# An attention block with two MLPs behind it on one core: plain scores in the first unit, earlier loads for the second, and scores between value products

## The chip, the core and the metric

The kernel runs on one core of a Trainium2 chip. The metric is the time of one execution in microseconds (us) on the device. TensorE (PE) multiplies matrices, VectorE (DVE), ScalarE (ACT) and GpSimd (POOL) work element by element, and SyncE (SP) issues most of the transfers between memory and the on-chip buffer.

## The reference, cut to what matters

Two batches of eight heads, 576 tokens, 64 columns a head, all in float32. The bias of the scores comes out of a small network over a function of the two positions. Two MLPs follow.

```
S = 576
scores = (1/8) * q @ k.T
x = log1p(|i - j|) / log1p(max(i, 1))
bias = relu(x @ w1 + b1) @ w2
attn = softmax(scores + bias)
out = attn @ v
x = out.reshape(1152, 512)
x = (silu(x @ w_gate) * (x @ w_val)) @ w_out
y = softplus(x @ w_in) @ w_out2
```

## The kernel before, in words

Every engine runs in the order in which the program is written (`manual_schedule` over all five), so the place of a line in the loops is its place in the queue of its engine. A product of more than one pass splits its operands into a rounded high part and the remainder, the low part (`high`, `low`, L185 to L191), and the products of the parts are added up.

**The bias stretch.** A loop over 36 rows of blocks makes the bias for all heads. `hidden(i)` writes four tiles `r` = relu of a slice of the table `G`, three on DVE and one on ACT (L256, L258). `second` multiplies them on PE into `pb` (L266). `keep` copies `pb` on ACT to a staging tile `st`, of which there are four, and SP stores it into the bias tiles, 288 KB a row (L278, L282; the first four rows in two halves each, L285). From row 6 on each turn of the loop also takes one step of the preparation of the first unit's K and Q (`prepare_k`, `prepare_q`: a cast, then a subtraction of the high part). At rows 23, 26, 31 and 33 (`EARLY`) it runs a slot of the attention loop.

**The attention loop.** A unit is a pair of heads of one batch; there are eight. A unit has nine slots, four for its first 256 queries (`sub` 0) and five for the other 320 (`sub` 1), and the fifth chunk mixes rows of both heads (`mix`). `run_slot` does this in order: `scores` of the slot's chunk on PE (four matmul instructions, L303); `gather`, the copies of an earlier slot's transposes out of PSUM; `biased` on DVE, which adds the bias and takes the extremum (L324); `softmax` of the chunk before (exp on ACT, L338; sums and reciprocals on DVE, L342, L343; the normalisation on POOL, L346); two steps of preparation for the next unit; `transposes` on PE (L373); and, when the last piece of an earlier sub is gathered, `values` of all its pieces in one burst on PE (L400: 20 matmul instructions for `sub` 0, 30 for `sub` 1). The transposes of a sub follow three slots behind its last scores (`LAG`).

**Loads.** `load_k` and `load_qv` issue a unit's loads on SP, with K and Q each copied twice, so that the two heads of a pair fill 128 rows. Those of the first unit stand ahead of the stretch. The second unit's K loads at the first slot (row 23), its Q and V at slot 4, the first one behind the stretch. The two mix tiles `m0`, `m1` are made behind the stretch, and POOL clears their last 64 columns (L551); they lie where buffers of the stretch were, so each memset waits for what last used its place.

Of the kernel before, what the change touches and what calls it, by code (L numbers as in the profile page):

```python
# [11 lines left out]
F32 = mybir.dt.float32  # L12
# [7 lines left out]
P = 128  # L20
# [9 lines left out]

BATCHES = ((0,), (1, 2), (3,)), ((0, 1), (2, 3), (4,))
# [7 lines left out]
EARLY = (23, 26, 31, 33)  # L39

# [58 lines left out]
def tile_kernel(ctx: ExitStack, tc, qT, kT, vS, wb, wg, wv, wo, wi, wo2, table, out):  # L99
# [4 lines left out]

    nc.scalar.preload_act_table_set("exp_and_others")
# [11 lines left out]
    slots(xp, "a", ("B11", "T1", "B21", "B22"))  # L117
# [7 lines left out]
    with ExitStack() as actx:  # L125
# [30 lines left out]
        def load(r, src, pr, b):  # L156
            for d in range(2):
                sp.dma_start(
                    out=r[D * d : D * (d + 1)], in_=src[b, 2 * pr : 2 * pr + 2].rearrange("h d s -> d h s")
                )  # L160

        def load_k(i):

            pr, b = UNITS[i]
            kr = bias[0][:, :2] if i > 2 else rawp.tile([P, 2, S], F32, tag="kr", name="kr")
            load(kr, kT, pr, b)
            return dict(i=i, pr=pr, b=b, kr=kr)

        def load_qv(u):
            pr, b = u["pr"], u["b"]  # L170
            if u["i"] == 1:
                u["qr"] = pairs[5].rearrange("p (a s) -> p a s", a=2)
            else:
                u["qr"] = qraw.tile([P, 2, S], F32, tag="qr", name="qr")
            load(u["qr"], qT, pr, b)
# [29 lines left out]

        def prepare_q(u, sub):
# [6 lines left out]
            sm = smp.tile([P, 4, 5], F32, name="sm")  # L213
            if sub == 0:
                parts = [(0, 0, 0, 256), (1, 256, 0, 256)]
                chunks = [(0, 0), (1, 0), (0, 1), (1, 1)]
            else:
# [3 lines left out]
                chunks = [(0, 0), (1, 0), ("mix",), (0, 1), (1, 1)]  # L221
            u[sub] = dict(u, sub=sub, qh=qh, ql=ql, chunks=chunks, sm=sm, es=[], last=[], at={})
# [52 lines left out]
        def keep(s, pb):  # L275
            c, t = divmod(s, 8)
            st = stp.tile([P, S], F32, name="st")
# [8 lines left out]

        def scores(u, n):

            sub, pr, kst = u["sub"], u["pr"], u["kst"]
# [9 lines left out]

            parts = [(t, a, o) for t in ("ql", "qh") for a, o in heads]  # L300
# [107 lines left out]
        def finish(u):  # L408

            if u["i"] == 4 and u["sub"] == 0:  # L410
# [46 lines left out]
        load_qv(units[0])  # L457
        chunks = [(i, sub, n) for i in range(2 * NP) for sub in range(2) for n in range(4 + sub)]
        jobs, turned, gathered, done, spare = [], [], [], [], itertools.cycle([False, True])
        prep = itertools.chain(prepare_k(units[0]), prepare_q(units[0], 0))  # L460
        before = None
        slot = 0

        def run_slot():
            nonlocal turned, done, prep, before, slot
            if slot < len(chunks):
                i, sub, n = chunks[slot]
                if n == 0:
                    for _ in prep:
                        pass  # L470
                    if sub == 0:
                        if i + 1 < 2 * NP:
                            units.append(load_k(i + 1))
# [38 lines left out]
            for _ in range(len(gathered) if last_job else max(ends, default=0)):  # L512
# [11 lines left out]
        with tc.manual_schedule(engines={E.PE, E.Activation, E.DVE, E.Pool, E.SP}):  # L524
# [7 lines left out]
            for i, s in enumerate(order):  # L532
# [6 lines left out]
                if i > 5:  # L539
                    next(prep, None)  # L540
# [7 lines left out]
            pairs[2:] = pairs[3:] + pairs[2:3]  # L548
# [528 lines left out]
```

## Time and profile before

| | |
|---|---|
| median of three runs | 601.92 us (600.58 to 603.95) |
| profiled execution | 600.55 us, its span 598.5 us |
| PE busy | 582.8 us, 97% of the span |
| DVE, ACT, POOL busy | 460.3, 376.2, 111.5 us |
| DMA | 63.30 MB, mean 106 GB/s |
| bias stretch | to about 64 us |
| attention with its last value burst | to 197.01 us |

The span is the time between the first and the last instruction in the profile of the one execution; the rest of its 600.55 us lies around it. Busy shares are means over all of it: the two MLPs, from 197 us on, are long rows of matmuls, and the attention part ahead of them is where the engines wait for each other.

### The profile page before, as it was taken

Reading aid. Unit: us, or ns where it says so; the run is one execution under the profiler, and the core shown is the slowest. Engines: PE = TensorE matmul, PEld = TensorE weight load, DVE = VectorE, ACT = ScalarE, POOL = GpSimd, SP = SyncE. Lnnn points to the kernel's source line nnn. Section 1 sums busy time; section 2 is a strip of 40 time slices with the busy share of each in tenths; the row PEclk is TensorE's granted clock in tenths of the full one; section 3 lists DMA queues with packets and bytes.
Section 4 is the critical chain, followed back from the end, with each engine's and each line's share of the span. In section 5 each row is a group of like instructions: output and inputs, shape, how many; then the busy total and the mean of one; then the engine's idle time right before and its main releaser. Section 6 shows DMA issues by size and latency. Waiting matters only on the chain.

```text
span 598.5 us, 11379 instructions
## 1 busy us (share of the span) xinstructions
PE 582.8 (97%) x4274; PEld 516.7 (86%) x4274; DVE 460.3 (77%) x982; ACT 376.2 (63%) x715; POOL 111.5 (19%) x165
## 2 busy tenths in 40 slices
PE   8899799999999999999999999999999999999997
PEld 6343588888887999999999999999989989988986
DVE  7999578878888999897689735679998976983432
ACT  5998787879888876665558424349835734732520
POOL 0301587878993000000000000000000000000000
PEclk9999999999999999999999999999999999999999
DMA  8979923334432333324225222122444240400012
GB/s 221 207 197 208 214 63 99 91 110 111 110 119 89 117 98 108 103 75 137 73 79 190 84 71 71 71 75 70 138 130 134 90 141 5 137 36 1 2 51 106
DMA packets 47414, 63.30 MB, mean 106 GB/s; under 512 B 4480, under 2 KB 35200, under 8 KB 47360
## 3 DMA queue, kind: packets, MB, share of 16 engines
q1 hardware_dynamic: 47360, 62.59, 36.7%
q8 instruction: 33, 0.54, 0.4%
q14 instruction: 21, 0.17, 0.1%
HBM read 49.60 MB, written 2.36 MB: 87 GB/s over the span
## 4 chain that ended last, share of the span: by engine, by line
PE 81%; DVE 7%; ACT 4%; DMA 4%; issue 2%; POOL 2%; SPq 0%; DVEq 0%; ACTq 0%; POOLq 0%
PE pw L684 37%; PE pw L992 16%; PE pw L635 13%; PE ps L303 5%; PE po L400 5%; PE pt L373 4%; DVE r L258 3%; DMA bias<-st 2%; ACT st L278 1%; DMA e<-in_qT_dram 1%; ACT r L256 1%; POOL ql L191 1%; PE pb L266 1%; ACT e L338 1%; DMA G<-in_table_dram 1%
## 5 line engine op out<-in xcount | busy, mean ns | idle before, releaser
L992 PE MATMUL pw<-oh,g2h 128*128 128x512 f32 x144 | 56.2, 390 | 0.0
L992 PE MATMUL pw<-oh,g2l 128*128 128x512 f32 x144 | 56.1, 390 | 0.0
L992 PE MATMUL pw<-ol,g2h 128*128 128x512 f32 x144 | 56.1, 389 | 0.0
L303 PE MATMUL ps<-kst,ql 128*128 128x288 f32 x160 | 49.3, 337 | 4.5 <-POOL ql L191 3.4
L266 PE MATMUL pb<-r,wb_sb 128*32 128x288 f32 x576 | 49.1, 412 | 4.4 <-ACT st L278 2.7
L258 DVE TENSOR_SCALAR r<-G 128x576 f32<-128x576 f32 x108 | 51.5, 553 | 0.1
L635 PE MATMUL pw<-gh,sh 128*128 128x384 f32 x144 | 48.4, 336 | 0.0
L635 PE MATMUL pw<-gh,sl 128*128 128x384 f32 x144 | 48.4, 336 | 0.0
L635 PE MATMUL pw<-gl,sh 128*128 128x384 f32 x144 | 48.3, 336 | 0.0
L266 PEld LDWEIGHTS pb<-r,wb_sb 128*32 128x32 f32 x576 | 20.3, 109 | 31.5 <-ACT st L278 11.5
L609 DVE SCALAR_TENSOR_TENSOR x<-raw,x 128x512 int32<-128x512 int32 x68 | 46.2, 686 | 0.9
L303 PEld LDWEIGHTS ps<-kst,ql 128*128 128x128 f32 x160 | 29.0, 188 | 16.3 <-DVE sm L324 5.7
L303 PE MATMUL ps<-kst,qh 128*128 128x288 f32 x160 | 42.6, 294 | 0.0
L324 DVE CUSTOM_DVE_ANT_0 e<-ps,bias 128x576 f32<-128x576 f32 x44 | 33.0, 749 | 9.0 <-PE ps L303 7.6
L346 POOL TENSOR_SCALAR e<-e,sm 128x576 f32<-128x576 f32 x44 | 34.1, 784 | 25.2 <-DVE sm L343 19.4
L380 ACT COPY at<-pt 128x512 f32<-128x512 f32 (+2 forms) x69 | 36.2, 547 | 3.6 <-PE pt L373 3.4
L338 ACT ACTIVATE e<-e,sm 128x576 f32<-128x576 f32 x44 | 34.3, 780 | 6.1 <-DMA vt<-in_vS_dram 3.4
L400 PE MATMUL po<-at,v 128*64 128x256 f32 (+3 forms) x384 | 36.8, 332 | 1.0 <-DVE at L380 0.8
L1030 DVE TENSOR_TENSOR acc<-pw,acc 128x512 f32<-128x512 f32 x27 | 17.5, 684 | 25.1 <-PE pw L992 25.1
L606 DVE TENSOR_SCALAR x<-x 128x512 int32<-128x512 int32 x68 | 28.7, 426 | 9.2 <-ACT x L605 5.0
L400 PEld LDWEIGHTS po<-at,v 128*64 128x64 f32 x384 | 26.6, 137 | 8.0 <-issue 1.7
L992 PEld LDWEIGHTS pw<-oh,g2l 128*128 128x128 f32 x144 | 27.0, 188 | 5.8
(272 smaller groups left out, 1678.2 us busy)
## 6 DMA issues: line engine op xcount, KB each, us to landing
raw<-in_wo_dram SPq DMA_DIRECT2D x28, 512.0 KB, 3.6
bias<-st SPq DMA_DIRECT2D x32, 288.0 KB, 4.7
raw<-in_wi_dram SPq DMA_DIRECT2D x16, 512.0 KB, 3.8
raw<-in_wv_dram SPq DMA_DIRECT2D x12, 512.0 KB, 4.2
raw<-in_wg_dram SPq DMA_DIRECT2D x12, 512.0 KB, 3.5
qr<-in_qT_dram SPq DMA_DIRECT2D x14, 288.0 KB, 4.1
v<-in_vS_dram SPq DMA_DIRECT2D x8, 384.0 KB, 3.4
bias<-in_kT_dram SPq DMA_DIRECT2D x10, 288.0 KB, 4.2
```

The costliest lines, as they stand in the source:

```text
L258: nc.vector.tensor_scalar(r, G[:, w0 : w0 + S], PB[:, n : n + 1], 0.0, op0=ALU.add, op1=ALU.max)
L266: nc.tensor.matmul(pb[32 * ct : 32 * ct + 32, hf, :HALF], W2, rs[ct][:, HALF * hf : HALF * (hf + 1)], start=True, stop=True,)
L303: nc.tensor.matmul(ps[:, hf, :HALF], u[t][:, o : o + P], kst[:, a, HALF * hf : HALF * (hf + 1)], start=i == 0, stop=i == len(parts) - 1,)
L324: nc.vector.tensor_tensor_reduce(out=e[:, :S].rearrange("p (a n) -> p a n", a=2), in0=ps[:, :, :HALF], in1=bt.rearrange("p (a n) -> p a n" ...
L338: nc.scalar.activation(e, e, AF.Exp, bias=sm[:, 0, n : n + 1], scale=-1.0, accum_out=sm[:, 1, n : n + 1])
L346: nc.gpsimd.tensor_scalar(e, e, sm[:, 3, i : i + 1], 1.0, op0=ALU.mult, op1=ALU.mult)
L380: marks[eng, u["i"], u["sub"]] = copy(at[:, :w], pt[:, :w]).ins
L400: nc.tensor.matmul(u["po"][D * a : D * (a + 1), o : o + n], v[:, D * t : D * (t + 1)], at[:, i : i + n], start=piece == 0 and o == 0, stop ...
L609: nc.vector.scalar_tensor_tensor(yi, lw, 29, yi, op0=ALU.logical_shift_right, op1=ALU.bitwise_or)
L635: nc.tensor.matmul(ps[:, :n], w[:, k], x, start=first and k == 0 and i == 0, stop=last and k == NK - 1 and i == 2)
L684: nc.tensor.matmul(ps[:, hf, :HALF], a[:, o + k], b[:, HALF * hf : HALF * (hf + 1)], start=start and k == 0 and i == 0, stop=k == 1 and i ...
L992: nc.tensor.matmul(ps, g, w.rearrange("p k f -> p (k f)"), start=f == 0 and i == 0, stop=f == 3 and i == 2)
```

## The change

Six edits, all in the attention part.

1. `wb` loads from ACT's queue ahead of everything, so SP's first load is the table.
2. The first unit's K and Q load as two whole tiles of 128 rows, the heads stacked, and nothing of it is split. `plain_scores` multiplies plain float32 with 64 rows for each head. Where the slot's chunk is of the pair's first head, the chunk of the second head is made with it and kept in `ahead` for the next slot.
3. Staging has eight tiles: at even rows a half of `early[0]` or `early[1]`, which lie in the memory of slots `B21` and `B22`; those slots are made later, in `finish` of the third unit.
4. The second unit's K loads at row 20, the first 256 columns of its Q at row 28, the other 320 columns and V at slot 4.
5. The bias loop no longer takes steps of a preparation.
6. `MIDDLE`: after the third piece of a value burst, the scores of the next chunk are issued, and the rest of the burst follows (where the next chunk is of the same sub).

```diff
@@
+MIDDLE = 2
+NEXT = (20, 28)
@@
+    wb_sb = const.tile([P, 34], F32, name="wb_sb")
+    nc.scalar.dma_start(out=wb_sb, in_=wb)
@@
-    slots(xp, "a", ("B11", "T1", "B21", "B22"))
+    slots(xp, "a", ("B11", "T1"))
@@ def load_k(i):
-            kr = bias[0][:, :2] if i > 2 else rawp.tile([P, 2, S], F32, tag="kr", name="kr")
-            load(kr, kT, pr, b)
+            if i == 1:
+                kr = early[3]
...
+            if i == 0:
+                for t, src in ((0, kT), (1, qT)):
+                    sp.dma_start(out=kr[:, t], in_=src[b, 2 * pr : 2 * pr + 2].rearrange("h d s -> (h d) s"))
+                u["qr"] = kr[:, 1]
+                kr = kr[:, 0]
+            else:
+                load(kr, kT, pr, b)
@@ def prepare_q(u, sub):
+            if u["i"] == 0:
+                u[sub] = dict(u, **job(sub))
+                return
@@
         stp = pool("stp", 4)
+        early = [xp.tile([P, 2, S], F32, tag=f"a{i}", name=f"early{i}") for i in range(4, 8)]
+        spare_st = [t[:, i] for t in early[:2] for i in range(2)]
@@
-        wb_sb = gp.tile([P, 34], F32, name="wb_sb")
-        sp.dma_start(out=wb_sb, in_=wb)
@@ def keep(s, pb):
-            st = stp.tile([P, S], F32, name="st")
+            i = order.index(s) % 8
+            st = stp.tile([P, S], F32, name="st") if i % 2 else spare_st[i // 2]
@@
+        def plain_scores(u, *ns):
...
+            for step in range(2):
+                for ps, _, heads in made:
+                    for a, o, m in heads:
+                        rows = slice(D * a, D * (a + 1))
+                        hf = (step + a) % 2
+                        nc.tensor.matmul(
+                            ps[rows if m == D else slice(None), hf, :HALF],
+                            u["qr"][rows, o : o + m],
+                            u["kr"][rows, HALF * hf : HALF * (hf + 1)],
+                            start=True,
+                            stop=True,
+                        )
+            return [(ps, bt) for ps, bt, _ in made]
@@ def finish(u):
+            if u["i"] == 2 and u["sub"] == 0:
+                slots(xp, "a", ("B21", "B22"))
@@ def run_slot():
-                        if i + 1 < 2 * NP:
+                        if 0 < i < 2 * NP - 1:
                             units.append(load_k(i + 1))
@@
-                        load_qv(units[i + 1])
+                        load_q(units[i + 1], slice(256 if i == 0 else 0, S))
+                        load_v(units[i + 1])
@@
-                got = scores(u, n)
+                if ahead:
+                    got = ahead.pop()
+                elif i == 0 and u["chunks"][n][0] == 0:
+                    got, then = plain_scores(u, n, n + 1)
+                    ahead.append(then)
+                else:
+                    got = scores(u, n)
@@
                 values(w, piece)
+                if j == MIDDLE and slot < len(chunks) and n < 3 + sub and not ahead:
+                    ahead.append(scores(u, n + 1))
@@ for i, s in enumerate(order):
-                if i > 5:
-                    next(prep, None)
+                if i == NEXT[0]:
+                    units.append(load_k(1))
+                if i == NEXT[1]:
+                    load_q(units[1], slice(0, 256))
@@
-            pairs[2:] = pairs[3:] + pairs[2:3]
```

On POOL, around the end of the bias stretch, the order before is this (`e` a chunk's weights, `m` a mix tile, `kst` and `ql` the split K and the low part of Q):

```order
L191 TENSOR_TENSOR kst<-kr,kst 64x288 x3
L191 TENSOR_TENSOR ql<-qr,qh 128x256 x2
L219 MEMSET qh 128x64
L220 MEMSET ql 128x64
L191 TENSOR_TENSOR ql<-qr,qh 128x320 x2
L346 TENSOR_SCALAR e_113<-e_113,sm 128x576 x2
L346 TENSOR_SCALAR e_114<-e_114,sm 128x576
L551 MEMSET m_965 128x64
L551 MEMSET m_967 128x64
L346 TENSOR_SCALAR e_114<-e_114,sm 128x576
```

and with the change:

```order
L401 TENSOR_SCALAR e_111<-e_111,sm 128x576 x2
L401 TENSOR_SCALAR e_112<-e_112,sm 128x576
L619 MEMSET m_917 128x64
L619 MEMSET m_919 128x64
L401 TENSOR_SCALAR e_112<-e_112,sm 128x576
L212 TENSOR_TENSOR kst<-early_131,kst 64x288 x3
L401 TENSOR_SCALAR e_909<-e_909,sm 128x576 x2
L212 TENSOR_TENSOR ql<-qr,qh 128x256 x2
```

The first unit's splits are gone; behind the second memset stand the same normalisations and splits of the second unit as before. The place that the second memset clears is now last read by the store of the last row (35) of the stretch; before, it was that of an earlier row.

On PE, a value burst of `sub` 0 (L400 before, L455 after; `vt` holds the last 64 rows of V) and the scores of the next slot, before:

```order
L400 MATMUL po<-at,v 64x256 x8
L400 MATMUL po<-at,vt_101 64x256 x2
L303 MATMUL ps<-kst,ql 128x288
L303 MATMUL ps<-kst,qh 128x288
```

and with the change:

```order
L455 MATMUL po<-at,v 64x256 x6
L358 MATMUL ps<-kst,ql 128x288
L358 MATMUL ps<-kst,qh 128x288
L358 MATMUL ps<-kst,ql 128x288
L358 MATMUL ps<-kst,qh 128x288
L455 MATMUL po<-at,v 64x256 x2
L455 MATMUL po<-at,vt_100 64x256 x2
```

Four score matmuls stand now between the third piece and the fourth; each such line of values is two instructions in the trace. There are 14 such bursts.

On SP, the end of the stretch before:

```order
L158 DMA kr<-in_kT_dram 64x2x576 x2
L282 DMA bias_92<-st 16x8x576 x4
L282 DMA bias_93<-st 16x8x576 x8
L158 DMA e_957<-in_qT_dram 64x2x576 x2
```

and with the change:

```order
L164 DMA early_131<-in_kT_dram 64x2x576 x2
...
L308 DMA bias_91<-early_129 16x8x576
L164 DMA qr<-in_qT_dram 64x2x256 x2
L308 DMA bias_91<-st 16x8x576
...
L164 DMA qr<-in_qT_dram 64x2x320 x2
```

The first 256 columns of the second unit's Q now stand ahead of seven of the stores; before, all of it stood behind the last.

## Rows read from the trace of the kernel before

**Rows 1.** Page, part 5: costliest groups: busy us, mean ns, idle before and releaser

```profile
L303 PE MATMUL ps<-kst,ql 128*128 128x288 f32 x160 | 49.3, 337 | 4.5 <-POOL ql L191 3.4
```

**Rows 2.** Busy time by stretch of the span (from:to, length, busy us, clock, DMA share, GB/s)

```profile
15.00:30.00 15.00, 13.17 (x146) 5.14 (x146) 14.94 (x30) 13.85 (x22) 4.71 (x7) 1.00 0.93 207
45.00:60.00 15.00, 13.54 (x146) 5.39 (x139) 14.97 (x34) 12.54 (x22) 2.83 (x3) 1.00 0.97 208
597.00:598.50 1.50, 0.00 (x0) 0.00 (x0) 0.00 (x0) 0.00 (x0) 0.00 (x0) 0.52 0.14 52
```

**Rows 3.** DMA queue of SP in time: start, us, line, issue, count

```profile
1.19 0.42 SPq L240 DMA_DIRECT2D G<-in_table_dram  x1
16.59 27.92 SPq L282 DMA_DIRECT2D bias<-st  x20
46.02 18.47 SPq L282 DMA_DIRECT2D bias<-st  x12
```

**Rows 4.** DMA issues in 30 to 44, and in 63.9 to 64.4: KB, us to landing

```profile
bias<-st SPq DMA_DIRECT2D x10, 288.0 KB, 3.9
...
bias<-st SPq DMA_DIRECT2D x1, 288.0 KB, 5.2
```

**Rows 5.** Chain of waits, 60 to 75 us: start, us, what

```profile
63.97 0.53 SPq L282
...
65.29 6.20 DMA e<-in_qT_dram
...
74.64 0.37 PE po L400 x2
```

**Rows 6.** Waits of ACT in the first 64 us: total, times, longest

```profile
ACT st L278 <- DMA bias<-st: 2.5, 2, 1.4
```

**Rows 7.** DVE in time, bias stretch and behind it

```profile
5.18 2.67 DVE L258 TENSOR_SCALAR r<-G 128x576 f32<-128x576 f32 x6
...
7.76 0.77 DVE L535 TENSOR_SCALAR G<-G,wb_sb 128x1064 f32<-128x1064 f32 x1
...
8.45 9.11 DVE L258 TENSOR_SCALAR r<-G 128x576 f32<-128x576 f32 x21
...
43.52 0.75 DVE L324 CUSTOM_DVE_ANT_0 e<-ps,bias 128x576 f32<-128x576 f32 x1
...
57.98 2.66 DVE L258 TENSOR_SCALAR r<-G 128x576 f32<-128x576 f32 x6
```

**Rows 8.** POOL in time, end of the bias stretch

```profile
65.94 0.15 POOL L551 MEMSET m<- 128x64 f32 x1 [1.21 <-DMA bias<-st]
...
69.40 1.47 POOL L346 TENSOR_SCALAR e<-e,sm 128x576 f32<-128x576 f32 x2
...
72.05 0.72 POOL L191 TENSOR_TENSOR ql<-e,qh 128x256 fp32r<-128x256 f32 x1 [1.18 <-DVE qh L187]
```

**Rows 9.** PE in time: a transpose behind GpSimd, the second unit's first scores

```profile
66.87 0.33 PE L373 MATMUL pt<-ident,e 128*128 128x128 f32 x1 [0.55 <-POOL e L346]
...
72.89 0.37 PE L303 MATMUL ps<-kst,ql 128*128 128x288 f32 x1 [3.25 <-POOL ql L191]
```

**Rows 10.** Chain of waits, 0 to 300 us: value bursts (L400) and scores (L303)

```profile
91.36 2.31 PE po L400 x20
93.67 0.72 PE ps L303 x4
...
94.83 0.54 PE ps L303 x4
...
107.96 2.31 PE po L400 x20
...
123.65 2.31 PE po L400 x20
...
173.36 2.31 PE po L400 x20
```

**Rows 11.** Waits of DVE, 74 to 197 us: total, times, longest

```profile
DVE e L324 <- PE ps L303: 7.6, 9, 1.4
```

More of the change, by code (lines that the diff above doesn't have):

```diff
@@ L164, in load_k, with load_q, load_v @@
             pr, b = UNITS[i]
-            kr = bias[0][:, :2] if i > 2 else rawp.tile([P, 2, S], F32, tag="kr", name="kr")
-            load(kr, kT, pr, b)
-            return dict(i=i, pr=pr, b=b, kr=kr)
-        def load_qv(u):
-            pr, b = u["pr"], u["b"]
[L171 to L175, printed above, removed]
+            u = dict(i=i, pr=pr, b=b)
+            if i == 1:
+                kr = early[3]
+            elif i > 2:
+                kr = bias[0][:, :2]
+            else:
+                kr = rawp.tile([P, 2, S], F32, tag="kr", name="kr")
+            if i == 0:
[5 more added lines that the diff above has]
+                load(kr, kT, pr, b)
+            u["kr"] = kr
+            return u
+        def load_q(u, cols=slice(None)):
+            if "qr" not in u:
+                u["qr"] = qraw.tile([P, 2, S], F32, tag="qr", name="qr")
+            load(u["qr"], qT, u["pr"], u["b"], cols)
+        def load_v(u):
+            pr, b = u["pr"], u["b"]
             v = u["v"] = vp.tile([P, 4, 3 * D], F32, name="v")
@@ L204, in prepare_k, with job @@
                 yield
+        def job(sub):
+            chunks = [(0, 0), (1, 0), ("mix",), (0, 1), (1, 1)] if sub else [(0, 0), (1, 0), (0, 1), (1, 1)]
+            return dict(sub=sub, chunks=chunks, sm=smp.tile([P, 4, 5], F32, name="sm"), es=[], last=[], at={})
         def prepare_q(u, sub):
             qr = u["qr"]
+            if u["i"] == 0:
+                u[sub] = dict(u, **job(sub))
+                return
             width = 704 if sub else 512
@@ L220, in prepare_q @@
                 nc.gpsimd.memset(ql[:, 320:384].bitcast(F32), 0.0)
-                chunks = [(0, 0), (1, 0), ("mix",), (0, 1), (1, 1)]
-            u[sub] = dict(u, sub=sub, qh=qh, ql=ql, chunks=chunks, sm=sm, es=[], last=[], at={})
+            u[sub] = dict(u, qh=qh, ql=ql, **job(sub))
             for j, (a, o, s0, w) in enumerate(parts):
@@ L285, in keep @@
                     sp.dma_start(out=bias[c][D * a + t : D * a + t + 61 : 4], in_=st[a::2])
+        def plain_scores(u, *ns):
+            sub, made = u["sub"], []
+            for n in ns:
+                ch = u["chunks"][n]
+                if ch[0] == "mix":
+                    heads, bt = [(0, 512, D), (1, 256, D)], bias[4][:, u["pr"]]
+                else:
+                    a, c = ch
+                    heads, bt = [(a, 256 * sub + D * (sub and a) + P * c, P)], bias[2 * sub + c][:, 2 * u["pr"] + a]
+                made.append((psS.tile([P, 2, 512], F32, tag="S", name="ps"), bt, heads))
+            for step in range(2):
[11 more added lines that the diff above has]
+            return [(ps, bt) for ps, bt, _ in made]
         def scores(u, n):
-            sub, pr, kst = u["sub"], u["pr"], u["kst"]
+            sub, pr = u["sub"], u["pr"]
             ch = u["chunks"][n]
@@ L456, in tile_kernel @@
         units, late = [load_k(0)], []
-        load_qv(units[0])
+        load_v(units[0])
         chunks = [(i, sub, n) for i in range(2 * NP) for sub in range(2) for n in range(4 + sub)]
         jobs, turned, gathered, done, spare = [], [], [], [], itertools.cycle([False, True])
-        prep = itertools.chain(prepare_k(units[0]), prepare_q(units[0], 0))
+        prep = prepare_q(units[0], 0)
         before = None
+        ahead = []
         slot = 0
@@ L511, in run_slot @@
             last_job = over and gathered and gathered[0][0] is units[-1][1]
-            for _ in range(len(gathered) if last_job else max(ends, default=0)):
+            for j in range(len(gathered) if last_job else max(ends, default=0)):
                 w, piece = gathered.pop(0)
                 values(w, piece)
+                if j == MIDDLE and slot < len(chunks) and n < 3 + sub and not ahead:
+                    ahead.append(scores(u, n + 1))
                 if piece == PIECES[w["sub"]][-1]:
```

11 lines of the change are left out of this document (7 added, 4 removed).

## Prediction

> **What bounds the kernel now.** I read the page first, then the stretches, then the queues in time. On the page TensorE is busy for 97% of the span, and the dense projections of the two MLPs hold most of it; the change doesn't touch them. TensorE's idle time that this change could give back is small: in front of the scores it is 4.5 us in all, 3.4 us of them behind GpSimd's `ql` [rows 1]. So the question is where the attention part (the first 197 us) ends, and there are two places. The first is the bias stretch, 5 to 64 us. Its engines stay full: VectorE is busy for 14.94 to 14.97 of each 15 us, and the DMA engines reach a share of 0.93 to 0.97 at 207 to 208 GB/s [rows 2]. Both are near a limit. Behind it TensorE stands still for 3.25 us, until the second unit's `ql` is there at 72.89 [rows 9]. The chain tells why: the last store is issued at 63.97, the query loads only behind it, and they need 6.20 us to land [rows 5]. The second place is the row of eight units. From the value burst at 74.64 to that at 173.36 [rows 5, 10] are six units in 98.72 us; the shortest step, 107.96 to 123.65, is 15.69 us, and the one before, from 91.36, is 16.60. Six steps of 15.69 would save 4.6 us: so much, and no more, can an earlier VectorE give back there.
>
> **The start and VectorE.** `wb` goes to ACT's queue and the table is first on SP's: an issue takes 0.42 us [rows 3], so the first `r` starts 0.42 us earlier, at 4.76. Without the first unit's casts and splits VectorE does 108 `r`, the long table step (0.69 us until the next `r`), and three evaluations of 0.75 us. At the undisturbed pace of 9.11/21 = 0.434 us a `r` [rows 7] that is 46.9 + 0.7 + 2.3, so the last `r` ends near 54.8, against 57.98 + 2.66 = 60.64 now. The last store was issued 3.3 us behind it (63.97); with that lag it would now be ready at 58.2.
>
> **The stores.** VectorE no longer decides, the DMA engines do. Now the first full store is issued at 16.59 [rows 3], after ACT once waited 1.4 us for a staging tile [rows 6]; with eight tiles that wait goes, so it is near 16.6 - 0.4 - 1.4 = 14.7. From there 32 stores and two K loads of 0.295 MB and two Q loads of 0.131 MB have to pass: 10.29 MB. At 208 GB/s [rows 2] that takes 49.5 us, and the last store lands at L = 64.2, against 63.97 + 5.2 = 69.2 now [rows 4, 5]. Lower end: the DMA engines keep up with VectorE, and the last store lands 3.9 us, the time of the middle of the stretch [rows 4], after 58.2, at 62.1. Upper end: the pace of now, 34 transfers from 16.6 to 69.2, 1.55 us each, and one load's bytes more: 35 × 1.55 from 14.7, 68.9. I take 64.2, since the queue's share is already 0.97 and a full queue's rate is the nearest row.
>
> **What L releases.** GpSimd's order decides here. The memset of the second mix tile lies on a staging tile and waits for the store of the last row; now it waited for an earlier one and ran at 65.94 [rows 8]. Behind it stand in both orders one normalisation, three lows of the second unit's K, two normalisations and the first `ql`. Now these run without a gap from 65.94 to 69.40 + 1.47 = 70.87; then GpSimd waits 1.18 us for Q, works 0.72, and TensorE begins 0.11 later [rows 8, 9]. In the change Q is there, so the second unit's scores start at L + (70.87 - 65.94) + 0.72 + 0.11 = L + 5.76: 69.96 instead of 72.89, a gain of **2.9 us**; by the ends of L from 5.0 gained to 1.8 lost. The first unit's splits that GpSimd drops are worth nothing by themselves: GpSimd has idle time all through the stretch, and that VectorE runs freer is already in its 0.434.
>
> **Plain scores.** A pair of chunks is 8 matmul instructions over 64 rows. By the column price of a value burst (2.31/20 = 0.116 us for 256 columns [rows 10]) they take 8 × 0.13 = 1.04 us, about what two chunks of 0.54 [rows 10] took; if the two heads don't run beside each other, 2.08. TensorE is busy for 13.2 to 13.5 of 15 us [rows 2], so the 1 us more lies in its idle time twice; the later pairs lie in its wait for GpSimd. I take nothing; 1 us lost is the upper end, nothing gained the lower, since that idle time is off the path.
>
> **Scores amid the value products.** Fourteen bursts are split after their third piece. What VectorE gains is that it need not wait so long for scores (7.6 us in nine waits [rows 11]); on the path at most the 4.6 us above. The cost: scores behind values take 0.72 us, scores behind transposes 0.54 [rows 10], so one change from values to scores costs 0.18, and each split has one more. Going back into values shows in no row by itself; the nearest is the first two value matmuls of a burst, 0.37 us [rows 5] where 2 × 0.116 would do, 0.14 more. So the cost lies between 14 × 0.18 = 2.5 and 14 × 0.36 = 5.0, and I take 14 × 0.27 = 3.8. Of the 4.6 I take 3.3, less than the whole because steps already at 15.69 have nothing to give: in sum **0.5 us lost**; ends: 2.1 gained (4.6 - 2.5) and 5.0 lost. The Trainium skill, "TensorEngine Tiling (Array Packing)", Key Properties, says that a change of tiling mode drains TensorE; scores use the whole array and values half of its columns, so by it both directions cost alike, and the splits would come to the 5.0. The 0.18 is such a drain in one direction; for the other no row decides.
>
> **The sum.** 2.9 gained, 0.5 lost: 2.4 us, from 600.55 (the profiled execution: span 598.5 and 2 us around it) to 598.15. The median of the three runs, 601.92, lies 1.37 above that execution, so I forecast **599.5 us**. About 0.5% (3.0 us) is what a measurement of this kernel can tell from no change. The forecast's own range is 597.4 to 602.0: from L = 62.1 with the same 0.5 lost (4.5 gained) to L = 64.2 with 3.0 lost in the splits.
>
> **Rivals.** (1) The DMA engines keep up: L = 62.1, 5.0 gained; the splits cost their lower end and all waits go, 2.1 gained: 7.1 in sum, 594.8. For it: in 30 to 44 us a store took 3.9 us to land [rows 4] although many were under way; against it: the share of 0.97. (2) Slower: the splits drain TensorE in both directions, and the fill behind a drain is a whole first pair, 0.18 + 0.37 = 0.55 us each, 7.7 us, with nothing given back because the waits at a unit's end are for GpSimd: 7.7 - 2.9 = 4.8 lost, 606.7. It decides from 0.21 us a split (2.9/14), and makes the kernel slower by 0.5% from 0.42. For it: a step of 15.69 stands there with the bursts whole, so VectorE's waits may be worth little; against it: 0.18 and 0.14 as read. (3) The clock falls: the last bias matmuls follow VectorE's last `r`, so TensorE has nothing left from about 60 (an estimate), and then waits until L + 0.9 for the normalisation behind the memset: some 5 us, longer than the 3.25 us of now [rows 9]; at the end of the program, with TensorE idle, it is 0.52 [rows 2], the lower level (1.2 GHz). If it falls here, the scores and transposes that follow that normalisation, now from 66.87 to the start of the wait at 72.89 - 3.25 = 69.64 [rows 9], 2.8 us, take 5.6; from L + 0.9 they end at L + 6.5, 0.8 us behind the GpSimd chain's L + 5.76, and the first matmuls after it may lose as much again: some 1.6 us, 601.1, no change. The Trainium skill, "TensorE: Matmul & The Clock Gate", Part 1, says that an idle TensorE falls to half rate. (4) The earlier loads don't matter because the memset comes as late as now (L = 68.9): 1.8 + 0.5 lost, 604.2, within the same bound.
>
> **How the numbers follow.** Forecast 0.39, rival (1) 0.37, rival (2) 0.15, clock 0.05, rival (4) 0.04. Faster by over 0.5%: rival (1), 0.37. Within 0.5%: forecast, clock and rival (4), 0.48. Slower: rival (2), 0.15. The range leaves out rival (2) and reaches from rival (1) to rival (4): 594.8 to 604.2.
>
> **What would show it.** In the changed profile: last `r` ending near 54.8; the memset of the second mix tile at L near 64.2; the second unit's first scores 5.8 us behind it, near 70, with GpSimd busy between; scores amid values at 0.72 us and the rest of a burst about 0.1 longer; steps of 15.7 to 16.0 us from one unit's burst to the next. Wrong it is if the last store lands before 63 or after 66, if the unit steps stay at 16.6 or grow, or if the clock falls near 65 us.

## The result and the profile after

The changed kernel is slower: 606.51 us (median of six runs, 606.2 to 607.31) against 601.72 (600.58 to 604.23), a ratio of 1.0084 with an interval of 1.0066 to 1.0102. The forecast was 599.5, within 594.8 to 604.2. The profiled execution took 606.64 us with a span of 604.9, 6.4 us more than the one before.

That is more than the 4.8 us between the medians: the profiled execution of the kernel before lies 1.2 us below its median. Two kernels of the experiments, e2 and e8, have its program up to the first value burst (e8 with one small tile elsewhere), and they began that burst at 76.11 and 76.31 us, not at 74.64, with a memset 0.4 to 0.6 us later and TensorE's clock fallen behind its wait (the last section). Against these the changed kernel's first burst is 0.6 to 0.8 us late, not 2.25.

Where the 6.4 us lie can be read from four marks: the first value burst, the first burst six units later, the start of the first MLP, and the end of the span.

| span time, us | before | after | difference |
|---|---|---|---|
| first value burst | 74.64 | 76.89 | +2.25 |
| six units, to the seventh burst of that kind | 98.72 | 103.59 | +4.87 |
| last bursts, to the start of the first MLP | 23.65 | 24.92 | +1.27 |
| both MLPs, to the end of the span | 401.5 | 399.5 | -2.0 |

**The stretch.** The windows of the changed kernel answer to [rows 2] (length, busy us of PE, PEld, DVE, ACT and POOL, clock, DMA share, GB/s):

```profile
0.00:15.00 15.00, 13.44 (x118) 8.69 (x120) 9.87 (x23) 9.28 (x13) 1.30 (x9) 1.00 0.56 184
15.00:30.00 15.00, 15.00 (x192) 7.39 (x190) 15.00 (x36) 15.00 (x25) 0.00 (x0) 1.00 0.96 209
45.00:60.00 15.00, 13.31 (x152) 6.30 (x144) 13.48 (x37) 14.15 (x27) 2.75 (x4) 1.00 1.06 204
60.00:75.00 15.00, 5.06 (x27) 3.29 (x24) 3.58 (x12) 3.34 (x8) 5.12 (x8) 0.66 0.79 156
```

The first 15 us of the kernel before:

```profile
0.00:15.00 15.00, 13.35 (x120) 9.02 (x120) 10.57 (x25) 8.79 (x12) 1.29 (x9) 1.00 0.88 221
```

In 15 to 30 us VectorE, ScalarE and TensorE are all full now, and the DMA engines move 204 to 209 GB/s without a pause from 15 us to the last landing, as costed. But in the first 15 us they are less used (0.56; before it was 0.88), and in the last window TensorE works for 5.06 of 15 us and its clock falls to a mean of 0.66. DVE in time answers to [rows 7], the queue of SP to [rows 3]:

```profile
5.09 0.30 DVE L596 TENSOR_SCALAR G<-G,wb_sb 128x144 f32<-128x144 f32 x1 [5.09 <-DMA wb_sb<-in_wb_dram]
...
5.88 2.67 DVE L283 TENSOR_SCALAR r<-G 128x576 f32<-128x576 f32 x6
...
53.16 2.66 DVE L283 TENSOR_SCALAR r<-G 128x576 f32<-128x576 f32 x6
```

```profile
16.30 0.55 SPq L308 DMA_DIRECT2D bias<-early  x1
...
59.14 0.55 SPq L308 DMA_DIRECT2D bias<-st  x1
```

VectorE starts 0.7 us later than before instead of 0.4 earlier: it waits for `wb`, whose load on ACT's queue lands at 5.09 here, behind the table (at 4.2 to 4.4 in the kernels below that load it so, and the `r` there start at 5.0 to 5.2, about as before). One of these, e1, has the same program up to there, so this lateness belongs to the execution, not to the change. The last `r` ends at 55.82, one us behind my 54.8; the last store is issued at 59.14, against 58.2. The first full store is issued at 16.30, against 14.7. Between that and the memset of the next rows, 53.4 us, 11.16 MB moved at 209 GB/s, and the last store needed 10.5 us to land. POOL and PE in time answer to [rows 8] and [rows 9]:

```profile
69.72 0.15 POOL L619 MEMSET m<- 128x64 f32 x1 [11.18 <-issue]
...
74.52 1.45 POOL L212 TENSOR_TENSOR ql<-qr,qh 128x256 fp32r<-128x256 f32 x2
```

```profile
70.66 0.48 PE L428 MATMUL pt<-ident,e 128*128 128x128 f32 x1 [9.94 <-POOL e L401]
...
75.33 0.40 PE L358 MATMUL ps<-kst,ql 128*128 128x288 f32 x1 [0.19 <-POOL ql L212]
```

The second memset runs at 69.72, when the last store is there (59.14 + 10.5 = 69.64; the row itself names no releaser); my L was 64.2. From it to the second unit's first scores it is 5.61 us (5.76 forecast), with GpSimd busy between, so that step held. TensorE waits 9.94 us for one normalisation.

**The units.** The chain of waits answers to [rows 10] (start, us, what):

```profile
76.89 1.45 PE po L455 x12
78.33 0.72 PE ps L358 x4
79.06 1.01 PE po L455 x8
80.07 0.59 PE pt L428 x4
80.66 0.53 PE ps L358 x4
...
86.36 1.76 PE po L455 x14
88.12 0.73 PE ps L358 x4
88.85 1.91 PE po L455 x17
90.76 1.02 PE pt L428 x8
91.78 0.53 PE ps L358 x4
...
180.48 1.45 PE po L455 x12
```

From a burst of the first 256 queries to the end of the second scores behind it, it is now 80.66 + 0.53 - 76.89 = 4.30 us; before, 94.83 + 0.54 - 91.36 = 4.01 [rows 10]. For the other 320 queries it is 91.78 + 0.53 - 86.36 = 5.95 us. The same place of the kernel before, by its chain:

```profile
84.04 3.04 PE po L400 x30
87.07 0.73 PE ps L303 x4
87.80 0.87 PE pt L373 x8
88.68 0.53 PE ps L303 x4
```

That is 88.68 + 0.53 - 84.04 = 5.17. So a split costs 0.29 us of TensorE's time in the one and 0.78 in the other, most of it in the products themselves: 1.76 + 1.91 instead of 3.04. VectorE's waits for scores [rows 11] did shrink, which the splits were to do:

```profile
DVE e L379 <- PE ps L358: 4.5, 6, 1.7
```

But TensorE now waits for VectorE. The six units, before and after, and TensorE's waits after:

```profile
74.64:173.36 98.72, 97.80 (x856) 84.27 (x858) 81.66 (x256) 82.63 (x203) 83.27 (x120) 1.00 0.35 93
```

```profile
76.89:180.48 103.59, 101.12 (x856) 83.91 (x858) 85.09 (x255) 83.06 (x201) 82.82 (x118) 1.00 0.34 91
```

```profile
PE ps L358 <- DVE sm L379: 2.5, 3, 0.9
```

TensorE was idle for 0.92 us of the 98.72 and is idle for 2.47 of the 103.59; its waits for `sm`, 0.4 us before, are 2.5. So 3.3 of the 4.87 us are more work on TensorE, and 1.55 are new waiting.

### The profile page after: what moved, and what is told of

It is laid out like the page before. It is cut to its first block, busy times and chain, and to the rows that moved or that the text cites. A ratio compares the mean times of both kernels' runs of the same rounds, so it can differ in the third digit from the quotient of the medians.

```text
span 604.9 us, 11363 instructions
## 1 busy us (share of the span) xinstructions
PE 584.2 (97%) x4274; PEld 514.0 (85%) x4274; DVE 458.7 (76%) x977; ACT 375.4 (62%) x713; POOL 104.4 (17%) x156
## 4 chain that ended last, share of the span: by engine, by line
PE 85%; ACT 6%; DVE 3%; DMA 3%; issue 1%; POOL 1%; DVEq 0%; POOLq 0%; ACTq 0%
PE pw L752 37%; PE pw L1060 16%; PE pw L703 12%; PE po L455 7%; PE ps L358 5%; PE pt L428 4%; DMA bias<-st 3%; PE pb L291 2%; ACT r L281 2%; DVE r L283 1%; ACT early L304 1%; ACT st L304 1%; ACT at L435 1%; PE warm L594 1%; ACT e L393 1%
## 5 line engine op out<-in xcount | busy, mean ns | idle before, releaser
L291 PE MATMUL pb<-r,wb_sb 128*32 128x288 f32 x576 | 47.5, 412 | 0.9 <-ACT st L304 0.7
L283 DVE TENSOR_SCALAR r<-G 128x576 f32<-128x576 f32 x108 | 47.3, 521 | 0.0
L435 ACT COPY at<-pt 128x512 f32<-128x512 f32 (+2 forms) x69 | 36.5, 550 | 14.7 <-PE pt L428 14.7
L358 PE MATMUL ps<-kst,ql 128*128 128x288 f32 x140 | 42.9, 335 | 2.7 <-DVE sm L379 2.5
L455 PE MATMUL po<-at,v 128*64 128x256 f32 (+3 forms) x384 | 43.2, 335 | 1.2 <-DVE at L435 1.1
L291 PEld LDWEIGHTS pb<-r,wb_sb 128*32 128x32 f32 x576 | 22.3, 109 | 25.4 <-DVE r L283 9.6
L428 PE MATMUL pt<-ident,e 128*128 128x128 f32 x188 | 31.9, 279 | 9.9 <-POOL e L401 9.9
L358 PE MATMUL ps<-kst,qh 128*128 128x288 f32 x140 | 37.3, 294 | 0.0
L428 PEld LDWEIGHTS pt<-ident,e 128*128 128x128 f32 x188 | 23.3, 142 | 15.2 <-POOL e L401 10.2
L455 PEld LDWEIGHTS po<-at,v 128*64 128x64 f32 x384 | 26.8, 136 | 9.6 <-issue 3.8
```

The costliest lines, as they stand in the source:

```text
L283: nc.vector.tensor_scalar(r, G[:, w0 : w0 + S], PB[:, n : n + 1], 0.0, op0=ALU.add, op1=ALU.max)
L291: nc.tensor.matmul(pb[32 * ct : 32 * ct + 32, hf, :HALF], W2, rs[ct][:, HALF * hf : HALF * (hf + 1)], start=True, stop=True,)
L358: nc.tensor.matmul(ps[:, hf, :HALF], u[t][:, o : o + P], kst[:, a, HALF * hf : HALF * (hf + 1)], start=i == 0, stop=i == len(parts) - 1,)
L428: nc.tensor.transpose(pt[:, P * w : P * (w + 1)], e, ident)
L435: marks[eng, u["i"], u["sub"]] = copy(at[:, :w], pt[:, :w]).ins
L455: nc.tensor.matmul(u["po"][D * a : D * (a + 1), o : o + n], v[:, D * t : D * (t + 1)], at[:, i : i + n], start=piece == 0 and o == 0, stop ...
```

## The experiments

Each kernel ran in three rounds beside the kernel before; times are medians. The kernel before had 602.38 us beside e1, e2, e3 and e7, 602.13 beside e4, e5, e6 and e8, and 603.33 beside e9 to e12, so a difference between kernels of two such groups, or from the changed kernel, is known to about 1 us.

**e1: the bursts whole.**

```diff
-MIDDLE = 2
+MIDDLE = 99
```

> The changed kernel with its value bursts left whole; all its other edits stay. Theory (the splits cost TensorE time: about 0.3 us in a burst of the first 256 queries, 4.30 against 4.01 us from its start to the second scores behind it, and about 0.8 us in one of the other 320, 5.95 against 5.17; little of it comes back): seven of each are 7.5 us, of which the steps from unit to unit showed 5.7, so 606.5 falls by 5 to 7 us, to 599.5 to 601.5, and the steps are 16.3 to 16.6 us. Rival (the time went in the bias stretch, where the last store lands at 69.6, and the splits pay for themselves): it stays within 1.5 us of 606.5.

Measured: 600.13 us, 6.4 less than the changed kernel; ratio to before 0.9958 (0.9944 to 0.9972). Its chain:

```profile
76.86 2.31 PE po L455 x20
...
175.71 2.31 PE po L455 x20
```

Six units in 98.85 us, those of before (98.72). The splits are the whole of the difference in the units, and without them the kernel is some 2 us faster than the kernel before; e8 shows where that comes from.

**e2: the kernel before with the splits alone.**

```diff
-                got = scores(u, n)
+                got = ahead.pop() if ahead else scores(u, n)
...
                 values(w, piece)
+                if j == MIDDLE and slot < len(chunks) and n < 3 + sub and not ahead:
+                    ahead.append(scores(u, n + 1))
```

> The kernel before with one edit alone, the scores of the next chunk behind the third piece of a value burst. Theory (splits cost 0.3 and 0.8 us): 5 to 7 us more than before, 606.7 to 608.7, with steps from unit to unit near 17.4 us. Rival (they pay for themselves): 601.7 within 1.5 us. The two MLPs take 401.5 us from the end of the attention part, as before, if their 399.5 in the changed kernel comes from where the buffers lie; 399.5 if it comes from the splits.

Measured: 608.93 us against 602.38, ratio 1.0103 (1.0074 to 1.0133).

```profile
76.11 2.76 PE po L402 x12
...
181.36 1.45 PE po L402 x12
```

105.25 us for six units. The first burst stood at the lower clock here (2.76 us instead of 1.45), which is 1.3 of it. The MLPs take 401.5 us, as before. So the splits cost some 6 us in either kernel, and the shorter MLPs come from something else.

**e3: only the bursts of 256 queries split.**

```diff
-                if j == MIDDLE and slot < len(chunks) and n < 3 + sub and not ahead:
+                if j == MIDDLE and w["sub"] == 0 and slot < len(chunks) and n < 3 + sub and not ahead:
```

> The changed kernel with only the bursts of the first 256 queries split; those of the other 320 stay whole. Theory (the two column halves of TensorE work beside each other in a burst; in a burst of 320 queries the first half of columns has more to do in the first pieces and the second half in the last ones, so a cut between them leaves each half idle once): most of the cost is in the 320s, so it falls by 4 to 5.5 us from 606.5, to 601 to 602.5. Rival (each split costs the same, the drain of TensorE and its fill): it falls by half of what whole bursts give, 2.5 to 3.5 us, to 603 to 604.

Measured: 602.71 us, 3.8 less than the changed kernel and 2.6 more than whole bursts.

```profile
75.29 1.45 PE po L455 x12
...
176.10 1.45 PE po L455 x12
```

100.81 us for six units: 2.0 more than whole, 0.33 a split, so nothing of the 0.29 comes back. TensorE's idle time in them is 0.81 us, so the new waiting comes with the 320s. The split of the 320s makes up the other 2.8 of six units, 0.46 each of the 0.78 that it costs on TensorE. The times lie between the two expectations; the larger share belongs to the 320s, as the theory says, but not by as much.

**e7: TensorE kept busy in its wait.**

```diff
             for w, e in enumerate(blocks):
+                if slot == 6 and w == 3:
+                    fill = psO.tile([P, 512], F32, name="po")
+                    for _ in range(36):
+                        nc.tensor.matmul(fill[:, :P], ident, ident, start=True, stop=True)
                 nc.tensor.transpose(pt[:, P * w : P * (w + 1)], e, ident)
```

> The changed kernel with 36 more matmuls of 128 columns, of no use, ahead of the transpose that waits for GpSimd from 60.7 to 70.7 us, so that TensorE is busy in most of that wait; its outputs stay the reference's. Theory (GpSimd's order behind the memset sets when the second unit's scores start, and the fallen clock, a mean of 0.66 in 60 to 75 us, hides behind it): the clock reads 1.00 in 60 to 75, those scores still start 5.7 us behind the memset, and the time stays within 1 us of 606.5. Rival (the fallen clock delays TensorE): 1.5 to 3 us less.

Measured: 605.67 us, 0.8 less. The window, then POOL and PE in time:

```profile
60.00:75.00 15.00, 12.55 (x105) 11.36 (x105) 5.21 (x17) 4.83 (x12) 7.09 (x11) 1.00 0.78 169
```

```profile
67.75 0.15 POOL L625 MEMSET m<- 128x64 f32 x1 [10.00 <-issue]
```

```profile
73.38 0.40 PE L360 MATMUL ps<-kst,ql 128*128 128x288 f32 x1 [1.73 <-POOL ql L214]
```

The clock is 1.00, and the scores start 5.63 us behind the memset all the same (5.61 with the fallen clock), now behind a wait of 1.73 us for `ql`. The memset itself ran at 67.75; in kernels with the same stretch it lay between that and 69.7. The first burst follows 7.18 us behind the memset (74.93), in the changed kernel 7.17 (76.89). So the fallen clock hid behind GpSimd's chain, and the 2.1 us between the two spans (602.8 and 604.9) are the earlier memset, not the clock.

**e4: the memset out of GpSimd's way.** The mix tile is cleared at slot 10; it is first written at slot 15.

```diff
             for i, mp in enumerate((tmpp, ep1)):
                 mixes.append(mp.tile([P, 5 * P], F32, name=f"m{i}"))
-                nc.gpsimd.memset(mixes[-1][:, S:], 0.0)
+                if i == 0:
+                    nc.gpsimd.memset(mixes[-1][:, S:], 0.0)
...
+            if slot == 10:
+                nc.gpsimd.memset(mixes[1][:, S:], 0.0)
```

> The changed kernel with whole value bursts, and GpSimd's clearing of the second mix tile moved behind the splits of the second unit's Q (the tile is first written five slots later). Theory (that memset, held until the last store lands near 69, holds everything behind it on GpSimd; without it only VectorE's evaluation of the chunk that reads the last bias rows waits): the splits of K and Q are done before 66, the second unit's scores start 1 to 1.5 us behind the last landing instead of 6, the first value burst starts near 73 instead of 76.9, and the time falls by 3 to 4 us from 600.1, to 596 to 597. Rival (the landing itself holds the path, through the bias rows, whatever GpSimd does): 600.1 within 1 us.

Measured: 598.07 us, 2.1 less than e1; ratio to before 0.9936 (0.9914 to 0.9959), whose interval meets that of e1. The spans are 595.4 and 598.8.

```profile
69.99 0.58 PE L358 MATMUL ps<-kst,ql 128*128 128x288 f32 x1 [5.78 <-DVE sm L379]
...
75.83 0.40 PE L358 MATMUL ps<-kst,ql 128*128 128x288 f32 x1
```

The place of the second row in the kernel before:

```profile
76.87 0.40 PE L303 MATMUL ps<-kst,ql 128*128 128x288 f32 x1
```

The scores start at 69.99 instead of 75.01, and wait for VectorE alone. By the program VectorE waits for the last bias rows, whose store lands at 68.6 (58.11 + 10.5); the trace names the load of Q's rest, which lands at 68.78. But now nothing hides the fallen clock (0.77 in 60 to 75 us): from the first scores to those behind the burst it takes 5.84 us, against 76.87 - 72.89 = 3.98 in the kernel before. Some 1.9 of the 4 to 5 us went there. The theory held in place, less in size.

**e5: Q's rest and V behind the third unit's K.**

```diff
-                        load_q(units[i + 1], slice(256 if i == 0 else 0, S))
-                        load_v(units[i + 1])
+                        if i:
+                            load_q(units[i + 1])
+                            load_v(units[i + 1])
...
                             units.append(load_k(i + 1))
+                        if i == 1:
+                            load_q(units[1], slice(256, S))
+                            load_v(units[1])
```

> The changed kernel with whole value bursts, and the second unit's last 320 columns of Q and its V (0.72 MB) loaded behind the third unit's K, which waits for a buffer until behind the stretch. Theory (these loads take a share of the DMA engines while the last stores are still under way): the memset that waits for the last store runs 2 to 3.5 us earlier than 69, near 66, and the second unit's scores as much; the time falls to 597 to 598.5, or less if Q comes late. Rival (the stores' own bytes and their start set the landing): the memset stays at 68 to 69.

Measured: 600.6 us, no difference from e1.

```profile
68.83 0.15 POOL L628 MEMSET m<- 128x64 f32 x1 [11.02 <-issue]
```

The memset stays. The theory fell: without these loads 10.64 MB moved in the 54 us from the first full store on, but at 196 GB/s, as if the loads used what the stores leave.

**e6: late memset, V late, `wb` on SP.** Without the splits; the memset's edit is that of e4, V's that of e5.

```diff
-    nc.scalar.dma_start(out=wb_sb, in_=wb)
+    nc.sync.dma_start(out=wb_sb, in_=wb)
```

> The changed kernel with whole value bursts and three more edits: the late clearing of the mix tile, the second unit's V loaded behind the third unit's K (Q stays where it is), and the weights of the bias network loaded by SP ahead of the table, as before the change. By the terms: VectorE's first step near 4.4 instead of 5.1 us, the last store lands 0.6 + 2 us earlier, near 66.5, the second unit's scores start near 67.5, the first value burst near 70.5 to 71.5, and the time is 594 to 596. Rival (the clock, fallen in TensorE's wait, takes half of it back): 597 to 598.

Measured: 597.27 us, as much as e4 within their spread. VectorE begins at 4.66, not earlier than in e4 (4.27), and the second unit's scores start at 70.91, not at 67.5; with the memset gone the third unit's K already loads at 63.08, ahead of the last landing. My terms for V and for the start gave nothing that can be seen. The time is the rival's, and the clock reads 0.77 in 60 to 75 us, as in e4; by how much that holds it back, this run does not show.

**e8: the small tile, in the kernel before.**

```diff
+    wb_sb = const.tile([P, 34], F32, name="wb_sb")
     nc.scalar.preload_act_table_set("exp_and_others")
...
-        wb_sb = gp.tile([P, 34], F32, name="wb_sb")
```

> The kernel before with one edit: the small tile of the bias network's weights (34 columns) lies in the pool that is opened first, as in the changed kernel; its load stays on SP. This moves all later tiles by its size. Theory (the two MLPs, 401.5 us from the end of the attention part before and 399.4 to 399.5 in every kernel with the change's layout, depend on where the tiles lie, and this tile is what moved them): 399.5, and the whole 2 us less than before, about 600. Rival (it comes from the later place of two of the split weights' tiles, or from another edit): 401.5, no change.

Measured: 600.24 us against 602.13, ratio 0.9973 (0.9959 to 0.9987). The longest piece of the MLPs in the chain of the kernel before:

```profile
199.04 127.77 PE pw L684 x960
```

and of e8:

```profile
200.77 126.68 PE pw L684 x960
```

The next longest takes 71.28 us before and 70.74 in e8. The MLPs take 399.4 us, 2.1 less, and the pieces have the lengths that they have in the changed kernel (126.74 and 70.74). Moving one tile of 34 columns to the first pool, which shifts every tile behind it, is the whole of the 2 us.

**e9: the second unit's loads at the start.** Whole bursts and the late memset of e4, and

```diff
         load_v(units[0])
+        units.append(load_k(1))
+        load_q(units[1], slice(0, 256))
...
-                if i == NEXT[0]:
-                    units.append(load_k(1))
-                if i == NEXT[1]:
-                    load_q(units[1], slice(0, 256))
```

> The changed kernel with whole value bursts, the late clearing of the mix tile, and the second unit's K and first 256 columns of Q (0.85 MB) loaded at the start, behind the first unit's V, where the DMA engines are busy for only 0.53 to 0.60 of 5 to 15 us, instead of at rows 20 and 28. Theory (the last store's landing, near 69, is set by the bytes that pass a full queue at some 205 GB/s from the first full store on): 0.85 MB less in that stretch are up to 4 us; with some delay of the first stores 2 to 3.5 us remain, so the second unit's scores start at 66.5 to 68 instead of 70.0, and the time is 594.5 to 596 against 598.1. Rival (the pace of the stores is set by SP's limit of transfers under way, not by bytes): within 1 us of 598.1.

Measured: **591.8 us** against 603.33, ratio 0.9825 (0.9788 to 0.9862): the fastest of all, faster than both kernels, and below the 594.5 to 596 expected. The queue of SP, PE in time, and two windows:

```profile
4.49 1.26 SPq L164 DMA_DIRECT2D early<-in_kT_dram  x2
```

```profile
65.36 0.37 PE L358 MATMUL ps<-kst,ql 128*128 128x288 f32 x1 [1.16 <-DVE sm L379]
```

```profile
0.00:15.00 15.00, 13.48 (x128) 9.24 (x132) 10.71 (x25) 10.03 (x15) 1.30 (x9) 1.00 0.91 257
60.00:75.00 15.00, 13.07 (x97) 10.59 (x97) 11.52 (x37) 11.56 (x29) 12.14 (x20) 1.00 0.74 143
```

The DMA engines are busy for 0.91 of the first 15 us instead of 0.56, the last store is issued at 57.08 and lands 7.0 us later, not 9.5 to 10.6, and the second unit's scores start at 65.36, 4.6 us before those of e4. TensorE's wait for them is down to 1.16 us, so the clock stays at 1.00 and the 1.9 us of e4 are not paid: 4.6 and 1.9 are 6.5, about the 6.3 us between the two times.

**e10: e9 with TensorE kept busy.** Fourteen matmuls as in e7, ahead of the scores of slot 9.

> The kernel of e9 with 14 more matmuls of 128 columns, of no use, ahead of the second unit's first scores, so that TensorE is busy in the middle of its wait; its outputs stay the reference's. Theory (after the wait the first scores and the first value burst run at the lower clock: in e4 5.8 us from the first scores to those behind the burst, where 4.0 us were needed before): the clock reads near 1.00 in 60 to 75 and the time is 1 to 2 us less than e9. Rival (the wait is by now too short for the clock to fall, or the lower clock is hidden): no difference from e9 within 0.7 us.

Measured: 592.22 us, no difference that counts. The clock was at 1.00 already, and the idle matmuls, 3.13 us, were longer than the wait that they were to fill: the first burst began at 68.59 instead of 67.08.

**e11: four staging tiles.** Whole bursts, and

```diff
-            i = order.index(s) % 8
-            st = stp.tile([P, S], F32, name="st") if i % 2 else spare_st[i // 2]
+            st = stp.tile([P, S], F32, name="st")
```

> The changed kernel with whole value bursts and only the four staging tiles of before. Theory (the bytes set the landing, so more staging only lets the issues run ahead of it): the last landing and the memset behind it stay within 1 us of 69, and the time within 1 us of 600.1. Rival (eight tiles are what keeps the DMA engines full): ACT waits for staging, the memset comes 2 us or more later, 602 or more.

Measured: 596.65 us, 3.5 less than with eight; neither expectation had that. ACT's waits for staging, and POOL:

```profile
ACT st L303 <- DMA bias<-st: 3.6, 4, 2.6
```

```profile
65.66 0.15 POOL L618 MEMSET m<- 128x64 f32 x1 [1.46 <-DMA bias<-st]
```

ACT waits 3.6 us for staging again, and the time is lower all the same, because the memset no longer stands on the tile of the last row: it waits for an earlier store and runs at 65.66, 3.3 us before that of e1 (68.97). The last landing itself did not move, as the theory had it: the last store is issued at 63.55 and lands 4.7 us later, at 68.3; in e1 at 68.9 (58.26 + 10.6). So the eight tiles let the issues run ahead and changed which store GpSimd waits for, and the second is the effect that shows in the time.

**e12: the split behind the first piece.**

```diff
-MIDDLE = 2
+MIDDLE = 0
```

> The changed kernel with all 14 splits, but behind the first piece of a burst instead of the third. Theory (in a burst of 320 queries one half of TensorE's columns gets 320 columns a piece and the other 192, and the second catches up in the last pieces; a cut behind three pieces makes it idle for three differences, one behind the first piece for one): the bursts of 320 cost 0.4 to 0.5 us of TensorE's time more than whole ones instead of 0.8, so 1.5 to 2.5 us less than 606.5, 604 to 605. Rival (a split costs its two drains wherever it lies): 606.5 within 0.7 us.

Measured: 616.73 us, 10.2 more than behind the third piece. TensorE's waits, 70 to 215 us, the first part of a 320 burst, and the second part of two:

```profile
PE ps L358 <- DVE sm L379: 10.9, 10, 2.0
```

```profile
85.56 0.75 PE L455 MATMUL po<-at,v 128*64 128x320 f32 x6
```

```profile
87.85 2.58 PE po L455 x26
...
106.73 4.23 PE po L455 x26
```

The part that the theory was about came out. The first part ends at 86.31, 0.68 us behind the transposes ahead of it (85.63), so the products take 0.68 + 2.58 = 3.26 us, against 3.67 behind the third piece and 3.04 whole. But the scores come too early now: there are two score tiles, and TensorE stands in the middle of the burst until VectorE has emptied one, 10.9 us in ten waits (2.5 in three in the changed kernel). Behind three of these waits the clock fell too (0.72 in 106 to 112 us, 0.76 in 143 to 150, 0.79 in 182 to 190), and the second parts there took 4.23, 4.23 and 3.90 us instead of 2.58. 8.4 us more waiting and 4.6 at the lower clock, less 7 x 0.41 of products, are 10.1 us, about the 10.2 measured. Neither I had counted, and they decide.

## Why the prediction was wrong

**The last landing, L = 64.2, was mis-sized: it was 69.7.** This was "From there 32 stores and two K loads of 0.295 MB and two Q loads of 0.131 MB have to pass". The start was 16.30, not 14.7, and from it to the memset 53.4 us passed, not 49.5. Of the start most is the late `wb`: in e1, with the same program up to there, it is 14.95, and the memset still runs at 68.97, 54.0 us behind it. So the larger part is the second, 3.9 to 4.5 us. The rate was right (209 GB/s), but 11.16 MB moved, not 10.29. Some 0.35 MB were already under way when I began to count, mostly of the first four rows; some 0.5 MB were loads behind the last store. e5 takes these loads away and its 10.64 MB need as long, 54.2 us, at 196 GB/s. So the 0.35 MB, 1.7 us, are shown; why the other 2.2 us or more stay without the loads is open. My upper end was 68.9, and I gave it 0.04. e9 shows the term from the other side: with 0.85 MB moved ahead of the first full store (15.32), it is 48.8 us to the last landing. VectorE, which does not decide here, ended its last `r` one us late (55.82; the terms add up to 54.7, not to the 54.8 written there). The step behind L, scores 5.76 us after the memset, held (5.61), so those scores came 2.4 us later than in the profiled execution before (75.33 and 72.89) instead of 2.9 earlier.

**"What L releases" had the sentence that mattered, and I drew too little from it.** I saw that the memset now waits for the last row's store and not for an earlier one, and priced it only as a matter of when L is. e11 and e4 show it as a loss of its own, 3.5 and some 2 us.

**The splits: 0.5 us lost was forecast, 6.1 came.** Two terms failed. The price: I took 14 equal splits at 0.27. In the bursts of 256 that is right (0.29), half by luck: the 0.14 for going back into values came from a row of [rows 5] that ends where its window ends, at 75 us, and so is a piece of a burst cut off by the view, not the time of two products.

In the bursts of 320 it is 0.78. The two heads of a pair lie in two halves of TensorE's columns, and the times fit if these halves work beside each other. A piece gives 2 x 320 columns to the one and 2 x (128 + 64) to the other, and the block `f` behind the fourth piece gives that other half the 1,024 that make both 2,560; the last piece gives 640 to each. A cut behind three pieces leaves 1,920 against 1,152, and behind it 1,280 against 2,048. A burst of 256 queries gives each half 2,560 columns in 2.31 us [rows 10]. At that pace the fuller halves need 1.73 and 1.85 us; measured are 1.76 and 1.91. One after the other, all columns at the pace of that burst's 5,120 would need 1.39 and 1.50. So one half idles for 768 columns before the cut and the other behind it; 768 are 0.69 us, and the products took 0.63 more (3.67 against 3.04). With the cut behind one piece it is 256 columns, 0.23 us, and they took 0.22 more (e12).

The gain: I took 3.3 us of 4.6. VectorE's waits did shrink, from 7.6 to 4.5 us, but the 4.6 were not idle time of TensorE, which stood for 0.92 us in the six units before; whole bursts give the same 98.85. What came back is 7 x (0.29 + 0.78) = 7.5 less the 6.1 of the two rows of the first table, 1.4 us, and in the 6.1 are 1.55 us in which TensorE waits for VectorE to empty a score tile, which no term of mine had.

Rival (2) had the place and the sign, 7.5 us on TensorE where it had 7.7. That its time came out (606.7; 606.5 measured) is luck: it counted 2.9 us gained in the stretch, and there was a loss, and it had nothing for the MLPs. Its mechanism was wrong: not a fill of 0.37 behind each drain, but two halves that no longer fit together. Of the drain that the Trainium skill names ("TensorEngine Tiling (Array Packing)", Key Properties), the bursts of 256 show 0.29 us for both directions, between my two prices, 0.18 and 0.36.

**The clock** fell, as rival (3) had it, and cost nothing in the changed kernel (e7), since GpSimd's chain is longer than what TensorE had to do at half speed; I had 1.6 us for it. In e1 the burst follows the memset by 7.89 us, not 7.17, with the scores at the lower clock, and where that chain is gone it costs 1.9 us (e4).

**Plain scores** took 1.24 us a pair (1.04 forecast) and lie beside other work, as said. They were not tried by themselves.

**The MLPs** I left out as untouched. The move of `wb`'s tile, which I costed only as a load, gave 2.0 us there (e8). With it the sum between the two profiled executions is +2.25 + 4.87 + 1.27 - 2.0 = 6.4 us.

## What to carry to other kernels

Where a memory's reuse makes an engine's small instruction wait for the last of a row of stores, move that instruction behind the work that doesn't need it: staging tiles and memory places set waits as much as data do. Where transfers are the bound, look for room in the windows before the stretch, not at its end: here bytes moved ahead of it were gained (e9), and bytes taken away behind it were not (e5). Before cutting a burst whose products fill two halves of TensorE's columns, add up the columns of each half on either side of the cut, and ask whether the buffer that the inserted work needs is free by then (e12).

## What the runs showed of the hardware

Where tiles lie in the on-chip buffer changes matmuls that touch none of the changed code: with a tile of 34 columns put in front, 960 matmuls of 288 columns take 126.7 instead of 127.8 us, and 408 of 384 columns 70.7 instead of 71.3, in every kernel with that layout. Why, no run here tells. TensorE's clock after the stretch differs between executions of nearly the same work: in the profiled execution of the kernel before it stayed at 1.00 behind the wait of [rows 9]; in e2, which is the same up to there, it read 0.93 in 60 to 75 us behind a wait of 3.48, and in e8 0.94 behind 3.47. The first three pieces of the burst took 2.76 instead of 1.45 us in e2, and the whole burst 2.52 instead of 2.31 in e8. The second seems to be the usual case: of 42 other executions of the kernel before, 41 have a mean granted clock of 0.994 to 0.997, and one has 0.999, as the profiled one has. What decides between the two, no run here tells.
